# Pool's breaks, and the buffers of output rows and row weights, in a one-core FFT and expert kernel

## The chip, the cores and the metric

The kernel runs on one core of a Trainium2 chip. The metric is device time in microseconds, the median of several executions. The core has five engines that run side by side and wait for one another by semaphores: TensorE (PE, matrix products into PSUM), VectorE (DVE), ScalarE (ACT), GpSimd (POOL, called Pool below) and SyncE (SP). SP issues most of the DMAs. Pool issues the indirect ones, whose target rows are read from a table of indices.

## The reference, cut to what matters

```python
X = np.fft.fft(np.fft.fft(x, axis=1), axis=2).real      # x: 8 x 2496 x 256
x = X.reshape(19968, 256)
logits = x @ w_gate                                     # 8 experts
e_idx = np.argmax(logits, axis=1)
gate_w = softmax(logits)[arange, e_idx]
eom = 1.0 / (1.0 + np.exp(-(x @ w_output_gate)))
for e in range(8):
    mask = e_idx == e
    h = np.maximum(x[mask] @ w1[e], 0.0)                # 256 -> 1024
    out[mask] = gate_w[mask, None] * eom[mask, e, None] * (h @ w2[e])   # 1024 -> 256
```

Each of 8 batches is transformed along both axes. Every resulting row goes to the one expert with the largest logit, through two matrix products, and back to its own place, scaled by its gate weight.

## The kernel before, in words

**The background** transforms the batches one by one: chunks of x are loaded (tile `xt`), folded on DVE, multiplied by tables on PE (`dstage`, line 546, and `sstage`, line 573), and gathered in one of two buffers, `rowbuf`. `gating` (line 640) picks the expert and the position of each row. Then `scatter` (line 736) writes the rows into a DRAM scratch, sorted by expert: 20 indirect DMAs of 128 rows for each batch, issued by Pool. Each row carries its weight and its token number behind its 256 values.

**The foreground** is 93 slots (`sched`, line 1224) of up to 256 rows of one expert. `load_x_` (line 1321) has SP load a slot's rows transposed (`xr`) and then its row weights and token numbers (`xf`, tile name of `f`, line 1329). `mm1` makes the hidden values in four parts g, `mm2` follows three parts later (LAG) and makes the output: ACT scales it into `y` (line 1469), and Pool writes `y` to the output rows by indirect DMA (line 1471), which reads the token numbers out of `f`. So a buffer of `y` and one of `f` are free again only when that DMA has landed. Slots 0 to 43 take rows of the first six batches (in groups that need 2, 4 and 6 batches); the others come after all 8. Loads run two slots ahead of the work. The first four slots (n < KS) multiply in float32: DVE first adds the two halves of `xr` into `x32` (line 1390, `x` in the rows), which every `mm1` of that slot reads. Later slots use float16 pairs, with the expert's weights split by `conv` (line 1354) on ACT and DVE.

**Order.** SP and Pool execute in the order in which the program emits their work (`PH1`, line 93), up to the point at which the background is through; there is one queue each, so an instruction that waits holds up all behind it. The order on PE, ACT and DVE is chosen by a planner when the program is built, by its own cost table and with the same buffer waits; on the chip it is fixed. On Pool the 20 scatters of a batch are interleaved with the outputs of the slots: those of the fourth batch between the outputs of slots 0, 1 and 2 (6, 6 and 8 of them, line 1474), later ones about four to a slot. Those of the eighth batch stand in a list that is emptied step by step (line 1554), and four DMAs of padding rows follow them.

**Pool's breaks.** Two kinds stand between its DMAs. `zeros` (line 438) is two additions on a tile of zeros; `breath` (line 443) calls it before a DMA when four (RUN) have gone by since the last break. The other is a one-element memset into a row of `rowbuf` that has just been scattered (line 747): it must wait until that scatter has landed. `pauses` (line 734) says behind which scatters it stands; it also starts the count of `breath` anew. Between the third and the fourth batch `zeros` follows every third scatter.

**Pools of buffers.** `fx` is a list of pools: one until the background is through, then two. So `bufs=4 * len(fx)` is 4 buffers first and 8 later. Tiles with one tag in one pool take its buffers in turn, in the order in which they are made. `y` has its tag with 2 buffers, `x32` one of its own with 1.

Of the kernel before, what the change touches and what calls it, by code (L numbers as in the profile page):

```python
# [12 lines left out]
F32 = mybir.dt.float32  # L13
# [30 lines left out]
BA = BAS[0]  # L44
# [43 lines left out]
BH = 4  # L88
# [166 lines left out]
def fft_moe_kernel(ctx: ExitStack, tc: tile.TileContext, xl, wg, w1, w2, tde, tdo, gt, ts0, tsm, tsr, tsq, cst, tid, out):  # L255
# [44 lines left out]
    def whole(p, m, h):  # L300
        t = p[0][m][h]
        return t if p is raw else t.rearrange("p a n -> p (a n)").bitcast(F32)

    if True:
# [335 lines left out]
        def gating(b):  # L640
# [90 lines left out]
                last["tid"] = nc.scalar.copy(r[:, :, 1].bitcast(I32), tidt[P, b * 20 + 4 * i:b * 20 + 4 * i + 4])  # L731
                yield

            pauses = ((9, 19), (19,))[b] if b < BA else (1, 5, 9, 13, 17) if b >= BH else ()

            def scatter(j):
                if b >= BH:
# [325 lines left out]
        def route(b):  # L1063
            for _ in gating(b):
                pass
# [74 lines left out]
        def steps():  # L1140
            fc = 6 * KC
            for n in range(5 * NB):
                b, i = divmod(n, 5)
                if i == 0 and b > BH:
                    add_gen(gating(b - 1))
# [51 lines left out]
                if b == BH:  # L1197
                    fold(n + 5)
                yield ("step", n)
            add_gen(gating(NB - 1))  # L1200
            while gens:
                for _ in piece("C"):
# [7 lines left out]
    if True:  # L1210
        fx = []
# [98 lines left out]
        def entry(n, k, hi):  # L1310
            rd, qi = sched[n][:2]
            t, w = (slots_a + [slots_b])[rd], (NAS + [NQ])[rd]
            return nc.sync.value_load(t[0:1, k * w + qi:k * w + qi + 1], min_val=0, max_val=hi)

        def early(k, i):
            i_ = getattr(i, "ins", i)
            tc.add_to_no_dep_group(f"early_read{k}", i_)
            tc.declare_no_dep(i_, group=f"late{k}", reason="rows of other batches")
            return i

        def load_x_(n):
            rd, qi, N, _, off, _ = sched[n]
            U = (N + 127) // 128
            need(rd)
            begun.add(rd)
            a = sl_[n] = {"U": U, "N": N, "wb": wof[n]}
            r = rowat[n] if n < 2 else entry(n, 1, DUM - off)
            x = a["x"] = fx[-1].tile([128, 4, 256], F16, name="xr", tag="xr", bufs=3 * len(fx))
            f = a["f"] = fx[-1].tile([128, 2, 2], F32, name="xf", tag="xf", bufs=4 * len(fx))
            H = UNIT if N <= UNIT else 128  # L1330
            rows = scr[ds(r + off if off else r, H * U), :]
            for i in (nc.sync.dma_start_transpose(x[:, :, 0:H * U], rows[:, 0:D].bitcast(F16)),
                      nc.sync.dma_start(f[0:H, 0:U], rows[:, D:RW].rearrange("(u p) w -> p u w", p=H))):
                if rd < LAST:
                    early(rd, i)
            return i
# [29 lines left out]
        def psum(tag):  # L1366
            if "old" not in psf:
                return psf["h"]
            turn[tag] += 1
            own, kept_there = {"h": (3, 2), "y": (2, 1)}[tag]  # L1370
            there = turn[tag] % (own + kept_there) >= own
            psf["hb"], psf["yb"] = (2, 1) if there else (3, 2)
            return psf["old"] if there else psf["h"]

        def halves(a, h):
            t = fx[-1].tile([128, 4, 256], F32, name="hc", tag="hc", bufs=3 * len(fx))
            a["h", h] = t
            a["hh", h], a["hl", h] = (v for v in t.rearrange("p f t -> p (f t)").bitcast(F16).rearrange("p (a f t) -> a p f t", a=2, f=4))

        def mm1(n, g):  # L1380
            a = sl_[n]
            T = slice(0, a["N"])
            if g % 2 == 0:
                halves(a, g // 2)
            ps = psum("h").tile([128, 2, 256], F32, name="hp", tag="h", bufs=psf["hb"])
            if n < KS:
                if g == 0:
                    a["x32"] = fx[0].tile([128, 2, 256], F32, name="x32", tag="x32", bufs=1)
                    with tc.issue_after(last["x32" if n else "rt"].ins):
                        last["x32"] = nc.vector.tensor_tensor(a["x32"], a["x"][:, 0:2], a["x"][:, 2:4], op=ALU.add)  # L1390
                w = whole((raw, wbuf)[n % 2], 0, g // 2).rearrange("p (k f) -> p k f", k=2)
                for k in range(2):
                    f = (2 * g + k) % 4
                    for kc in range(2):
                        last["mm"] = nc.tensor.matmul(ps[:, k, T], w[:, kc, f * 128:(f + 1) * 128], a["x32"][:, kc, T], start=(kc == 0), stop=(kc == 1))
                last["hl"] = nc.scalar.activation(a["h", g // 2][:, 2 * (g % 2):2 * (g % 2) + 2, T], ps[:, :, T], AF.Relu)
                return
            w1v = wbuf[a["wb"]][0][g // 2].rearrange("p a (k f) -> p a k f", k=2)
            for k in range(2):
                f = 2 * g + k  # L1400
                m = 0
                for kc in range(2):
                    for hl, x in ((0, kc), (0, 2 + kc), (1, kc)):
                        last["mm"] = nc.tensor.matmul(ps[:, k, T], w1v[:, hl, kc, (f % 4) * 128:(f % 4 + 1) * 128], a["x"][:, x, T], start=(m == 0), stop=(m == 5))  # L1404
                        m += 1
            G = slice(2 * (g % 2), 2 * (g % 2) + 2)
            hh, hl = a["hh", g // 2], a["hl", g // 2]
            nc.scalar.activation(hh[:, G, T], ps[:, :, T], AF.Relu)  # L1408
            last["hl"] = nc.vector.scalar_tensor_tensor(hl[:, G, T], ps[:, :, T], 0.0, hh[:, G, T], op0=ALU.max, op1=ALU.subtract)  # L1409

        def mm2(n, g):
            a = sl_[n]
            U, h = a["U"], g // 2
            M = min(128, a["N"])
            if g == 0:
                a["yp"] = psum("y").tile([128, 2, 256], F32, name="yp", tag="y", bufs=psf["yb"])
                a["y"] = fx[0].tile([128, 2, 256], F32, name="y", tag="y", bufs=2)
                a["ys"] = fx[0].tile([128, 2], F32, name="ysc", tag="ysc", bufs=2)
            u = g % 2 if U == 2 else 0
            if n < KS:  # L1420
# [56 lines left out]

        def experts():
            chained(load_x_, 0)
            chained(load_x_, 1)  # L1480
            for h in range(2):
                conv(0, 0, h)
# [4 lines left out]
            for n in range(NS + 1):  # L1487
                while due <= n + (4 if LAST in ready else 2):
                    chained(load_x_, due)
                    due += 1  # L1490
# [5 lines left out]
                for g in range(4):  # L1496
                    if n < NS:
                        mm1(n, g)
                        yield "h"

                    k, j = divmod(4 * n + g - LAG, 4)
                    if 0 <= k < NS:
                        mm2(k, j)
                        yield "y"
# [66 lines left out]
    def need(i):  # L1571
        while i not in ready:
            next(bg, None)
# [66 lines left out]
```

## Time and profile before

| | |
|---|---|
| median of 3 runs | 1088.9 us (1084.75 to 1096.11) |
| the profiled execution | 1094.69 us, span 1092.9 us, mean granted clock 0.99 |
| PE busy | 1053.3 us, 96% of the span |
| DVE busy | 782.8 us, 72% |
| ACT busy | 700.0 us, 64% |
| Pool busy | 443.0 us, 41% |

The busy time of an engine is the time in which an instruction of it was executing; matrix products are pipelined and their ends are modelled, so that a PE that is busy throughout may still run at a lower clock. The granted clock is told as a share of full speed. What an engine waited for is inferred from semaphore events; a Pool DMA's own time is that of its issue, and its landing is later.

### The profile page before, as it was taken

How to read it: one execution, taken by the hardware profiler on the slowest of the kernel's cores; microseconds unless marked ns; L12 is line 12 of the kernel's file. 1: busy time of each engine (PE TensorE's matmuls, PEld its weight loads, DVE VectorE, ACT ScalarE, POOL GpSimd, SP SyncE). 2: the span in 40 equal slices, each digit the busy share in tenths (PEclk: the TensorE clock that was granted, in tenths of full speed). 3: DMA queues.
4: the chain of work that ended last, by engine and by line, in shares of the span. 5: the costliest groups of instructions: out<-in, count | busy, mean ns of one | idle time of the engine just before them, and what ended most of it. 6: DMA issues, size and time to landing. Idle time of an engine off the chain costs nothing.

```text
span 1092.9 us, 27037 instructions
## 1 busy us (share of the span) xinstructions
PE 1053.3 (96%) x9946; PEld 938.5 (86%) x9946; DVE 782.8 (72%) x1583; ACT 700.0 (64%) x1247; POOL 443.0 (41%) x435
## 2 busy tenths in 40 slices
PE   7979999989999999989988999999999999999997
PEld 6867888878999999978877888899999888888886
DVE  7877875889997585895443545588767778788873
ACT  3986765656876565545434554577767677778772
POOL 0067786723466645656554221231222222232322
PEclk9999999999999999999998999999999999999999
DMA  9947799855457555558568625697988988899820
GB/s 358 405 172 283 240 395 310 295 162 158 135 155 187 142 156 152 138 152 205 142 170 196 154 45 132 198 294 242 286 222 250 253 222 218 239 267 246 223 63 30
DMA packets 167388, 226.53 MB, mean 207 GB/s; under 512 B 117077, under 2 KB 117849, under 8 KB 167254
## 3 DMA queue, kind: packets, MB, share of 16 engines
q1 hardware_dynamic: 151046, 179.94, 59.4%
q0 software_dynamic: 16208, 44.85, 11.8%
q8 instruction: 78, 1.28, 0.5%
q14 instruction: 56, 0.46, 0.1%
HBM read 183.89 MB, written 43.80 MB: 208 GB/s over the span
## 4 chain that ended last, share of the span: by engine, by line
PE 72%; DMA 7%; issue 6%; POOL 6%; ACT 4%; DVE 4%; another core or an unknown queue 0%; POOLq 0%; SPq 0%; DVEq 0%; ACTq 0%
PE hp L1404 31%; PE yp L1442 30%; PE psb_t L600 6%; POOL scr L740 3%; PE psb_t L555 2%; DMA scr<-rowbuf,desti 2%; DMA xt<-in_xl_dram 2%; POOL out_dram L1471 1%; POOL ztile L440 1%; PE yp L1437 1%; DMA tstr<-in_tsr_dram 1%; DMA xt<-in_w_dram 1%; DMA out_dram<-y,xf 1%; PE psb_t L559 1%; ACT xt L414 0%
## 5 line engine op out<-in xcount | busy, mean ns | idle before, releaser
L1404 PE MATMUL hp<-xr,w0b 128*128 128x256 f16 (+5 forms) x4272 | 449.6, 256 | 8.6 <-DVE hc L1409 8.6
L1442 PE MATMUL yp<-w1b,hc 128*128 128x256 f16 x3480 | 431.8, 274 | 5.0 <-ACT y L1469 4.7
L1404 PEld LDWEIGHTS <-w0b 128*128 128x128 f16 x4272 | 365.7, 98 | 52.7 <-DVE hc L1409 9.7
L1471 POOL DMA_INDIRECT out_dram<-y,xf x166 | 200.9, 1210 | 454.0 <-ACT y L1469 407.8
L1442 PEld LDWEIGHTS <-hc 128*128 128x128 f16 x3480 | 337.4, 98 | 45.8 <-issue 5.2
L1408 ACT ACTIVATE hc<-hp 128x512 f16<-128x512 f32 (+6 forms) x356 | 184.2, 526 | 127.4 <-PE hp L1404 119.3
L1409 DVE SCALAR_TENSOR_TENSOR hc<-hp,hc 128x512 f16<-128x512 f32 (+6 forms) x356 | 209.1, 600 | 71.9 <-ACT hc L1408 65.9
L1361 DVE SCALAR_TENSOR_TENSOR w1b<-raw1b,ssc,w1b 128x1024 f16<-128x1024 f32 x124 | 160.3, 1292 | 76.4 <-ACT w1b L1360 61.7
L740 POOL DMA_INDIRECT scr<-rowbuf,desti x160 | 179.9, 1124 | 73.9 <-issue 53.9
L1361 DVE SCALAR_TENSOR_TENSOR w0b<-raw0b,ssc,w0b 128x1024 f16<-128x1024 f32 x124 | 159.8, 1289 | 65.7 <-ACT w0b L1360 44.9
L1360 ACT ACTIVATE w0b<-raw0b,ssc 128x1024 f16<-128x1024 f32 x124 | 141.9, 1146 | 45.5 <-PE hp L1404 31.8
L1360 ACT ACTIVATE w1b<-raw1b,ssc 128x1024 f16<-128x1024 f32 x124 | 141.9, 1145 | 31.8 <-PE yp L1442 15.2
L1469 ACT ACTIVATE y<-yp,ysc 128x256 f32<-128x256 f32 x145 | 61.1, 470 | 59.9 <-PE yp L1442 31.9
L555 PE MATMUL psb_t<-tdet,ft 128*125 128x290 f32 (+1 forms) x240 | 65.6, 427 | 5.7 <-DVE eo L627 2.8
L555 PEld LDWEIGHTS psb_t<-tdet,ft 128*125 128x125 f32 (+1 forms) x240 | 46.1, 197 | 21.1 <-issue 3.4
L440 POOL TENSOR_TENSOR ztile<-ztile 128x256 f32<-128x256 f32 x70 | 53.2, 761 | 4.6 <-DMA scr<-ztile,pidx 1.4
L600 PE MATMUL psb_t<-amid,tstq 125*128 125x145 f16 (+3 forms) x480 | 48.0, 255 | 2.7 <-ACT w0b L414 2.7
L1448 DVE TENSOR_SCALAR ysc<-xf,ssc 128x2 f32<-128x2 f32 (+5 forms) x89 | 19.8, 223 | 28.0 <-DMA xf<-scr 15.3
L475 DVE TENSOR_TENSOR xt<-xt 128x500 f32<-128x500 f32 (+1 forms) x40 | 27.1, 680 | 15.5 <-DMA xt<-in_xl_dram 11.6
L637 ACT COPY rowbuf<-rowbuf 128x508 f16<-128x508 f16 x40 | 24.5, 614 | 21.0 <-DVE rowbuf L634 14.8
L634 DVE TENSOR_TENSOR rowbuf<-rt,rowbuf 128x516 f16<-128x516 f32 x40 | 28.6, 716 | 12.2 <-ACT rowbuf L633 6.7
L600 PE MATMUL psb_t<-amid,tst 128*128 128x145 f16 (+2 forms) x320 | 32.2, 251 | 2.5 <-ACT amid L567 2.5
(234 smaller groups left out, 843.1 us busy)
## 6 DMA issues: line engine op xcount, KB each, us to landing
raw0b<-in_w_dram SPq DMA_DIRECT2D x130, 512.0 KB
raw1b<-in_w_dram SPq DMA_DIRECT2D x130, 512.0 KB
xt<-in_xl_dram SPq DMA_DIRECT2D x40, 512.0 KB
xt<-in_w_dram SPq DMA_DIRECT2D x16, 512.0 KB
w0b<-in_w_dram SPq DMA_DIRECT2D x6, 512.0 KB
w1b<-in_w_dram SPq DMA_DIRECT2D x6, 512.0 KB
out_dram<-y,xf POOLq DMA_INDIRECT x166
scr<-rowbuf,desti POOLq DMA_INDIRECT x160
```

The lines of the kernel that those rows point to most:

```text
L440: nc.gpsimd.tensor_tensor(ztile[:, 0:D], ztile[:, 0:D], ztile[:, 0:D], op=ALU.add)
L555: last["ds"] = nc.tensor.matmul(o[:, 0:290], ft[:, j, par, W], tdw[:, j], start=(j == 0), stop=(j == 1))
L600: last["pe"] = nc.tensor.matmul(ps[:, k, c0:c0 + 145], tab[hl][K, t], a[K, kc, par, c0:c0 + 145], start=(n == 0), stop=(n == len(terms) - 1))
L740: free_order("scr", batch=b, inst=nc.gpsimd.indirect_dma_start(out=scr[:, :], out_offset=bass.IndirectOffsetOnAxis(ap=desti[:, j:j + 1], a ...
L1360: nc.scalar.activation(w[:, 0], r, AF.Copy, scale=sc)
L1361: nc.vector.scalar_tensor_tensor(w[:, 1], r, sc, w[:, 0], op0=ALU.mult, op1=ALU.subtract)
L1404: last["mm"] = nc.tensor.matmul(ps[:, k, T], w1v[:, hl, kc, (f % 4) * 128:(f % 4 + 1) * 128], a["x"][:, x, T], start=(m == 0), stop=(m == 5))
L1408: nc.scalar.activation(hh[:, G, T], ps[:, :, T], AF.Relu)
L1409: last["hl"] = nc.vector.scalar_tensor_tensor(hl[:, G, T], ps[:, :, T], 0.0, hh[:, G, T], op0=ALU.max, op1=ALU.subtract)
L1442: nc.tensor.matmul(a["yp"][0:M, u], a[k, h][:, f, u * 128:u * 128 + M], w2v[:, hl, f], start=(g == 0 and f == 0 and m == 0), stop=(h == 1 ...
L1469: nc.scalar.activation(a["y"][0:M, u], yp, AF.Copy, scale=ys[0:M, u:u + 1])
L1471: free_order("out", nc.gpsimd.indirect_dma_start(out=out[:, :], out_offset=bass.IndirectOffsetOnAxis(ap=a["f"].bitcast(I32)[0:M, u, 1:2], ...
```

## The change

Four lines are edited. From the fifth batch on there are no memsets behind scatters, so the only breaks are those of `breath`, one pair of additions before every fifth DMA. `f` has 8 buffers from the start. `y` has 3 buffers, and `x32` now takes its buffers from the same tag: for the first slots the buffers are taken in the order x32 of slot 0, y of slot 0, x32 of slot 1, y of slot 1, x32 of slot 2 and so on, with three in turn. So x32 of slot 2 takes the buffer that held y of slot 0, and x32 of slot 3 that of y of slot 1.

```diff
-            pauses = ((9, 19), (19,))[b] if b < BA else (1, 5, 9, 13, 17) if b >= BH else ()
+            pauses = ((9, 19), (19,))[b] if b < BA else ()
...
-            f = a["f"] = fx[-1].tile([128, 2, 2], F32, name="xf", tag="xf", bufs=4 * len(fx))
+            f = a["f"] = fx[-1].tile([128, 2, 2], F32, name="xf", tag="xf", bufs=8)
...
-                    a["x32"] = fx[0].tile([128, 2, 256], F32, name="x32", tag="x32", bufs=1)
+                    a["x32"] = fx[0].tile([128, 2, 256], F32, name="x32", tag="y", bufs=3)
...
-                a["y"] = fx[0].tile([128, 2, 256], F32, name="y", tag="y", bufs=2)
+                a["y"] = fx[0].tile([128, 2, 256], F32, name="y", tag="y", bufs=3)
```

Here BA is 2, BH is 4 and KS is 4; the batches count from 0.

## Rows read from the trace of the kernel before

**Rows 1.** The page: busy time by engine, and the chain that ended last.

```profile
PE 1053.3 (96%) x9946; PEld 938.5 (86%) x9946; DVE 782.8 (72%) x1583; ACT 700.0 (64%) x1247; POOL 443.0 (41%) x435
PE 72%; DMA 7%; issue 6%; POOL 6%; ACT 4%; DVE 4%; another core or an unknown queue 0%; POOLq 0%; SPq 0%; DVEq 0%; ACTq 0%
```

**Rows 2.** Busy us (instructions) of each engine by stretch; granted clock, DMA share, GB/s.

```profile
225.00:250.00 25.00, 21.72 (x166) 17.84 (x165) 21.74 (x53) 14.93 (x26) 5.62 (x4) 0.93 0.52 158
...
575.00:600.00 25.00, 22.51 (x179) 18.74 (x179) 10.38 (x14) 11.11 (x18) 9.88 (x11) 0.86 0.85 197
...
625.00:650.00 25.00, 25.00 (x231) 22.41 (x230) 13.03 (x18) 12.35 (x18) 4.93 (x4) 1.00 0.31 55
```

**Rows 3.** ACT's timeline, 440 to 600 us: start, us, [idle before, releaser].

```profile
525.36 0.84 ACT L1469 ACTIVATE y<-yp,ysc 128x256 f32<-128x256 f32 x2 [0.71 <-PE yp L1442]
...
576.60 0.84 ACT L1469 ACTIVATE y<-yp,ysc 128x256 f32<-128x256 f32 x2 [6.56 <-DMA out_dram<-y,xf]
...
598.86 0.84 ACT L1469 ACTIVATE y<-yp,ysc 128x256 f32<-128x256 f32 x2 [0.71 <-PE yp L1442]
```

**Rows 4.** Waits, 460 to 600 us: us in total, times, longest.

```profile
ACT y L1469 <- DMA out_dram<-y,xf: 15.9, 5, 6.6
...
DVE ysc L1448 <- DMA xf<-scr: 14.7, 5, 7.0
...
SPq L1333 <- DMA out_dram<-y,xf: 80.2, 10, 13.6
```

**Rows 5.** PE's timeline, 540 to 600 us.

```profile
577.49 6.49 PE L1442 MATMUL yp<-w1b,hc 128*128 128x256 f16 x32 [3.65 <-ACT y L1469]
```

**Rows 6.** Pool's instructions by line and form: busy us, mean ns, idle before.

```profile
L1471 POOL DMA_INDIRECT out_dram<-y,xf x166 | 200.9, 1210 | 454.0 <-ACT y L1469 407.8 <-issue 18.3 <-DMA raw0b<-in_w_dram 7.3
L740 POOL DMA_INDIRECT scr<-rowbuf,desti x160 | 179.9, 1124 | 73.9 <-issue 53.9 <-DVE desti L708 16.5 <-DVE r_t L824 1.1
L440 POOL TENSOR_TENSOR ztile<-ztile 128x256 f32<-128x256 f32 x70 | 53.2, 761 | 4.6 <-DMA scr<-ztile,pidx 1.4
...
L747 POOL MEMSET rowbuf<- 1x1 f32 x23 | 2.0, 88 | 74.4 <-DMA scr<-rowbuf,desti 74.4
```

**Rows 7.** Pool's timeline, 120 to 420 us.

```profile
148.95 0.99 POOL L740 DMA_INDIRECT scr<-rowbuf,desti  x1 [0.16 <-issue]
...
153.98 0.99 POOL L740 DMA_INDIRECT scr<-rowbuf,desti  x1 [0.15 <-issue]
...
162.95 0.97 POOL L1471 DMA_INDIRECT out_dram<-y,xf  x1 [0.30 <-ACT sq L513]
...
182.49 1.39 POOL L1471 DMA_INDIRECT out_dram<-y,xf  x1 [0.30 <-issue]
```

**Rows 8.** All engines' timeline, 223 to 240 us.

```profile
229.49 0.69 DVE L475 TENSOR_TENSOR xt<-xt 128x512 f32<-128x512 f32 x1 [2.35 <-DMA xt<-in_xl_dram]
...
238.19 2.19 PE L1404 MATMUL hp<-xr,w0b 128*128 128x256 f16 x11 [3.01 <-DVE hc L1409]
```

**Rows 9.** The chain that ended last, in order of time: start, us, what.

```profile
219.43 5.18 DMA out_dram<-y,xf
...
574.06 2.43 DMA out_dram<-y,xf
```

**Rows 10.** DVE's timeline, 125 to 232 us.

```profile
159.14 0.68 DVE L1390 TENSOR_TENSOR x<-xr 128x512 f32<-128x512 f16 x1
```

**Rows 11.** PE's timeline, 125 to 235 us.

```profile
161.22 1.89 PE L1395 MATMUL hp<-x,raw0b 128*128 128x256 f32 x8
...
183.60 1.94 PE L1395 MATMUL hp<-x,w0b 128*128 128x256 f32 x8
```

**Rows 12.** All engines' timeline, 484 to 520 us.

```profile
516.78 1.72 DVE L1361 SCALAR_TENSOR_TENSOR w1b<-raw1b,ssc,w1b 128x1024 f16<-128x1024 f32 x1 [0.64 <-issue]
...
517.43 2.23 POOL L440 TENSOR_TENSOR ztile<-ztile 128x256 f32<-128x256 f32 x2
```

**Rows 13.** The page: the costliest groups, mean ns of one.

```profile
L1361 DVE SCALAR_TENSOR_TENSOR w1b<-raw1b,ssc,w1b 128x1024 f16<-128x1024 f32 x124 | 160.3, 1292 | 76.4 <-ACT w1b L1360 61.7
```

## The prediction

> **What bounds the kernel now.** I read the page first. PE is busy for 96% of the span and holds 72% of the chain that ended last; Pool holds 6% and DMAs 7% [rows 1]. So a change can win only what PE idles or runs slowly, about 40 us of idle time (1092.9 minus 1053.3), and only where Pool or a landing DMA causes it. The table by stretch shows where. From 600 us on PE is full: 231 products in 25 us, 108.2 ns each; 575 to 600 us has 179 at a mean granted clock of 0.86, and 225 to 250 us has 0.93 [rows 2].
>
> The reader's key rows are ACT's scalings into `y`. A slot has 96 products, so it should take 96 x 108.2 ns = 10.39 us. Between the scalings at 525.36 and 598.86 us there are six slots in 73.50 us [rows 3], where 62.3 would do: 11.2 us are lost. The waits name the cause: between 460 and 600 us ACT waits 15.9 us for output DMAs to land (one of the two `y` buffers must come free), SP stands 80.2 us at the load of `xf` for the same landings (one of four `f` buffers), and DVE waits 14.7 us for the `xf` that SP loads late [rows 4]. At 577.49 us this reaches PE: it stands for 3.65 us, and its next 32 products take 6.49 us where 32 x 0.1082 = 3.46 are due [rows 5]. That is the lower of its two clock levels (1.2 GHz) for most of them, after an idle stretch.
>
> Pool is late because of what a slot costs it. Four scatters and two outputs take 6 x (1.15 in the mean + the 0.30 that stands before each) = 8.7 us, a pair of additions 1.5 us, and a landing wait with its memset (74.4 + 2.0)/23 = 3.3 us: 13.5 us, against PE's 10.39 [rows 6, 7]. Earlier slots are stretched by background work on PE and leave Pool time; from about 500 us on they are not.
>
> **The change, part by part.**
>
> *The landing waits.* Of the 23 memsets 20 go (five for each of four batches); they cost Pool some 20 x 3.3 = 66 us. What comes instead: 80 scatters, 4 pads and about 50 outputs of slots 6 to 30 stand under the count, and one pair for four DMAs makes 33 pairs, where the trace has 20 in that stretch: 13 more, 13 x 1.52 = 20 us. A slot's six DMAs with 1.5 pairs then take 8.7 + 2.5 = 11.2 us by the means. By Pool's undisturbed pace it is less: three scatters and a pair take 5.03 us (148.95 to 153.98) without any landing wait [rows 7], so a pair adds 5.03 - 3 x 1.28 = 1.2 us, and a slot takes 7.7 + 1.8 = 9.5 us. Against 10.39 Pool stays level or falls back by 0.8 us a slot for the six slots in which the last 24 scatters and pads are interleaved, 5 us in all.
>
> *Third `y` buffer, eight `f` buffers.* These 5 us are covered: a third buffer gives an output one more slot, 10.4 us, to land, and eight buffers of `f` give four more slots. Without that cover the 5 us would come back at ACT. So the ACT, SP and DVE waits of [rows 4] should go, and with them the 11.2 us: I take **-11**. Bounds: -7 if Pool's lag still costs two slots 2 us each, and -14.5 if a loss of about 3.5 us before 500 us, which PE has behind DVE, goes as well. Next late is then PE itself.
>
> *`f` again, at 220 us.* The load of slot 7's `xf` waits for the output of slot 3, which landed 5.18 us after its issue at 219.43 [rows 9]. The chunks of x queued behind it on SP come late: DVE stands 2.35 us for one at 229.49, and PE stands 3.01 us behind DVE at 238.19 [rows 8], at a mean clock of 0.93 around it, worth 0.07 x 25 = 1.8 us [rows 2]. With eight buffers nothing waits there. Bounds -2.4 (what DVE waited) and -4.8; I take **-3**, near the DVE wait, since DVE stays behind with other work.
>
> *`x32` in `y`'s tag.* This adds a wait. DVE's addition of slot 2 ran at 159.14 us [rows 10]; now it must wait until slot 0's output has landed. Pool issues the second half of that output at 162.95, behind the third batch's scatters [rows 7], which the change leaves alone. Outputs land 2.43 to 5.18 us after their issue [rows 9], here at 165.4 to 168.1. With 0.68 for the addition, slot 2's first product can start at 166.1 to 168.8 instead of 161.22 [rows 11]: 4.9 to 7.6 us later. Slot 3 waits likewise for slot 1's output, issued until 182.49 [rows 7]: 185.6 to 188.4 instead of 183.60, 2.0 to 4.8 us. Behind the addition stand DVE's folds and evictions for batches 4 and 5, and PE waits for those too. But PE has slot 1's second product and the background's tables in the same stretch, and the planner knows of the wait and can put them first. Lower end 0 (covered), upper end 7.6 plus 3.0 for the low clock afterwards = 10.6. I take **+4**, nearer to the covered end.
>
> *More additions beside DVE.* A weight split that met a pair took 1.72 us [rows 12], where its mean is 1.29 [rows 13]. Thirteen pairs at 0.43 are 5.6 us of DVE's time. In the Pool-bound stretch DVE is busy for 10.38 of 25 us [rows 2], which hides it there. Bounds 0 and 2 on PE; I take **+0.5**. The Trainium skill, page "SBUF — State Buffer", section "Who interferes with whom", says that a DVE instruction with two SBUF inputs contends with a GpSimd instruction that reads SBUF, and that whoever comes second is blocked for the whole instruction. By that rule the additions speak against this change; the rows agree that both lengthen, but show a third of the full block.
>
> **Sum.** -11 - 3 + 4 + 0.5 = -9.5. The profiled execution took 1094.69 us, so its like would take 1085.2. It lies above the median of 1088.9 and within the runs' spread; I count from the median: **1079.4 us**, rounded 1079.
>
> **The rivals.**
>
> 1. *The early wait eats the gain.* The planner's idea of when slot 0's output lands is wrong on the chip, the order is fixed, and PE stands 7.6 us and then runs slowly: -14 + 10.6 + 0.5 = -3, 1086 us. For it: Pool is in scatters until just before 162.95 us [rows 7], and DVE's queue holds the background's work too. Against: the fillers named. 0.18.
> 2. *Slower: both waits in full.* Slots 2 and 3 both stand, 7.6 + 4.8, with 3.0 of low clock after each: +18.4, so -14 + 18.4 + 0.5 = +5, 1094 us. It decides once the two stalls exceed 13.5 us together. Against: if slot 2 slips, slot 3 is due later and its wait is partly over. 0.13.
> 3. *More than forecast.* The early wait is covered, and the 3.5 us before 500 us go too: -14.5 - 4.8 + 0.5 = -19, 1070 us. 0.15.
> 4. *Additions block DVE fully.* If 13 x 1.52 = 20 us of DVE reach PE in the stretches where DVE is nearly full: -14 + 4 + 20 = +10, 1099 us. It is the rule of "SBUF — State Buffer" in the Trainium skill taken at its word. Against: the 1.72 above, and DVE's 72% [rows 1]. 0.04.
> 5. *Pool stays the bound.* Issues lengthen without landing waits, or landings do, and half of the late loss stays: -5.5 - 3 + 4 + 0.5 = -4, 1085 us. Against: the pace of 5.03 us for three scatters and a pair without a landing wait [rows 7]. 0.05.
>
> **How the numbers follow.** The forecast has 0.45, with its own range from 1074 to 1085 (the bounds of its terms, not all at one end). Rivals 3, 1, 2, 5 and 4 follow with the chances given. The range 1068 to 1095 takes in 1 to 3 and 5 and leaves out rival 4, the far ends and surprises of a newly planned order, under 2 in 10. About 1% is what a measurement of this kernel can tell from no change, 1078.0 to 1099.8 here. Faster than that: rival 3 and about half of the forecast, 0.15 + 0.23, with a little of the others 0.40. Slower: half of rival 4, the tail of rival 2 and a bad new order, 0.07. Within: 0.53.
>
> **What would show it.** Right, if ACT's wait for output DMAs and SP's at the load of `xf` between 460 and 600 us fall to near zero; if slots from 500 us on come every 10.4 us and the granted clock there is 1.00; if Pool shows idle time before outputs, waiting for ACT, where it now has landing waits; and if the stop at 238 us shrinks. The early step shows in DVE's addition of slot 2: later than 165 us with PE still full around it if covered, PE idle for 5 us or more, with a clock below 1, if not. Wrong, above all, if PE's busy time between 150 and 200 us falls by over 8 us, or if Pool's output DMAs still trail ACT by more than two slots at 560 us.

## The result, and the profile after

The changed kernel took **1077.07 us** in the median (1075.33 to 1079.06), the kernel before 1090.24 beside it (1084.75 to 1096.11). The ratio is **0.987**, with an interval from 0.983 to 0.9911. The forecast was 1079, so time and range held; the reasons held only in part. The profiled execution took 1076.54 us with a span of 1074.7: 18.2 us less than the span before. The medians differ by 13.2 only, because the profiled run of before lies 4.5 us above its median.

The page of after, busy time by engine and the chain that ended last [rows 1]:

```profile
PE 1047.2 (97%) x9946; PEld 937.2 (87%) x9946; DVE 776.2 (72%) x1583; ACT 703.0 (65%) x1247; POOL 408.7 (38%) x375
...
PE 89%; DVE 4%; ACT 3%; DMA 2%; issue 1%; POOL 0%; SPq 0%; POOLq 0%; DVEq 0%; ACTq 0%
```

Pool has left the chain (6% before), DMAs hold 2% of it instead of 7%, and PE holds 89%. Pool has 60 instructions fewer, which comes back below. The table by stretch of after, with the same columns as [rows 2]:

```profile
225.00:250.00 25.00, 24.27 (x201) 20.92 (x200) 24.55 (x61) 16.87 (x27) 4.12 (x4) 1.00 0.45 129
575.00:600.00 25.00, 25.00 (x230) 22.17 (x229) 11.38 (x15) 12.21 (x18) 4.93 (x4) 1.00 0.71 161
625.00:650.00 25.00, 25.00 (x232) 22.40 (x230) 13.25 (x17) 12.89 (x19) 5.82 (x5) 1.00 0.30 83
```

Both weak stretches are mended: 201 products at a granted clock of 1.00 where there were 166 at 0.93, and 230 where there were 179 at 0.86. ACT's timeline of after, the scalings of the same three slots as [rows 3]:

```profile
517.40 0.84 ACT L1469 ACTIVATE y<-yp,ysc 128x256 f32<-128x256 f32 x2 [0.71 <-DMA scr<-rowbuf,desti]
...
570.31 0.47 ACT L1469 ACTIVATE y<-yp,ysc 128x256 f32<-128x256 f32 x1 [0.71 <-PE yp L1442]
...
580.79 0.47 ACT L1469 ACTIVATE y<-yp,ysc 128x256 f32<-128x256 f32 x1 [0.71 <-PE yp L1442]
```

The six slots take 63.39 us instead of 73.50. Of the waits between 460 and 600 us, the rows of [rows 4] are gone; PE, Pool and SP's queue now head their lists with these, in total, times, longest:

```profile
PE hp L1404 <- DVE hc L1409: 0.5, 1, 0.5
...
POOL out_dram L1471 <- ACT y L1469: 63.9, 13, 8.5
...
SPq L1351 <- DVE w1b L1361: 33.2, 12, 5.3
```

Pool waits for ACT, as forecast, and SP's queue for weight buffers. Pool by line and form, for [rows 6]:

```profile
L1471 POOL DMA_INDIRECT out_dram<-y,xf x166 | 206.9, 1246 | 551.4 <-ACT y L1469 509.2 <-DMA raw0b<-in_w_dram 8.6 <-ACT w1b L1360 7.9
L740 POOL DMA_INDIRECT scr<-rowbuf,desti x160 | 173.1, 1082 | 64.7 <-issue 43.7 <-DVE desti L708 16.5 <-DVE rt L631 1.1
L440 POOL TENSOR_TENSOR ztile<-ztile 128x256 f32<-128x256 f32 x30 | 21.2, 705 | 1.5
...
L747 POOL MEMSET rowbuf<- 1x1 f32 x3 | 0.3, 88 | 4.7 <-DMA scr<-rowbuf,desti 4.7
```

Here is the surprise. The 20 memsets went, but **so did 40 of the 70 additions** [rows 6]: from the fifth batch on Pool has no break at all. The code says why. `breath()` puts a pair in where `run["n"] == RUN` while `run["on"]` is set, and then counts on. Outputs count too, also before `run["on"]`. Before, a memset set the count back to 0 now and then; now it has passed four when `run["on"]` is set, and never equals four again. The prediction had counted 33 pairs, 13 more than before.

The span by stage, in us, from ACT's scalings as above (slots counted from 0; the step from slot 8 to 9 is left out), for all kernels but noadds and bare, which the next section explains with the others:

```
            slot 0   0-4    4-5    5-8   9-20   20-26  26-32  32-end
before      154.28  70.46  18.38  54.79  146.31  67.57  73.50  494.07
after       155.81  68.10  13.99  55.48  146.31  64.07  63.39  493.88
y_only      158.81  68.88  16.39  55.26  146.66  66.49  68.36  494.02
f_only      161.92  70.25  13.84  55.34  147.75  68.34  71.34  494.10
fy          159.16  68.69  13.81  55.59  146.80  68.92  65.42  494.01
p_only      156.65  68.71  16.75  55.80  157.24  67.77  64.73  494.43
p_again     155.10  69.47  17.44  54.99  156.36  70.87  64.82  494.22
pf          156.41  70.25  13.71  55.68  146.31  64.07  63.40  493.95
py          156.42  67.52  18.14  54.86  146.31  64.08  63.40  493.90
p_breaks    157.17  70.24  17.10  54.76  148.87  67.46  63.40  493.94
breaks      158.49  68.68  13.71  56.82  148.88  66.05  63.39  493.87
x32_wait    163.11  69.97  15.03  53.84  157.98  70.12  64.06  494.00
```

Each row is one execution. The first column and 0-4 vary by several us between kernels that stand alike there; 9-20 and 26-32 repeat closely (146.31 in four kernels, 63.39 or 63.40 in five), so single microseconds are read from those two above all.

### The profile page after: what moved, and what is told of

Read it like the earlier page. It is cut to its first block, busy times and chain, and to the rows that moved or that the text cites. A ratio compares the mean times of both kernels' runs of the same rounds, so it can differ in the third digit from the quotient of the medians.

```text
span 1074.7 us, 26981 instructions
## 1 busy us (share of the span) xinstructions
PE 1047.2 (97%) x9946; PEld 937.2 (87%) x9946; DVE 776.2 (72%) x1583; ACT 703.0 (65%) x1247; POOL 408.7 (38%) x375
## 3 DMA queue, kind: packets, MB, share of 16 engines
q8 instruction: 78, 1.28, 0.5%
## 4 chain that ended last, share of the span: by engine, by line
PE 89%; DVE 4%; ACT 3%; DMA 2%; issue 1%; POOL 0%; SPq 0%; POOLq 0%; DVEq 0%; ACTq 0%
PE hp L1404 36%; PE yp L1442 34%; PE psb_t L600 7%; PE psb_t L555 3%; PE yp L1423 3%; PE hp L1395 2%; DMA xt<-in_xl_dram 1%; PE yp L1437 1%; DMA raw1b<-in_w_dram 1%; DVE xt L475 1%; DVE rowbuf L634 1%; PE psb_t L559 0%; ACT rowbuf L637 0%; PE psb_t L557 0%; DVE rt L631 0%
## 5 line engine op out<-in xcount | busy, mean ns | idle before, releaser
L1471 POOL DMA_INDIRECT out_dram<-y,xf x166 | 206.9, 1246 | 551.4 <-ACT y L1469 509.2
L740 POOL DMA_INDIRECT scr<-rowbuf,desti x160 | 173.1, 1082 | 64.7 <-issue 43.7
L555 PEld LDWEIGHTS psb_t<-tdet,ft 128*125 128x125 f32 (+1 forms) x240 | 45.1, 192 | 18.2 <-ACT rowbuf L637 3.3
L475 DVE TENSOR_TENSOR xt<-xt 128x500 f32<-128x500 f32 (+1 forms) x40 | 27.0, 680 | 13.2 <-DMA xt<-in_xl_dram 13.1
L637 ACT COPY rowbuf<-rowbuf 128x508 f16<-128x508 f16 x40 | 24.5, 613 | 18.3 <-DVE rowbuf L634 18.2
L633 ACT CAST rowbuf<-rt 128x516 f16<-128x516 f32 x40 | 25.0, 624 | 6.3 <-DMA scr<-rowbuf,desti 3.2
L600 PEld LDWEIGHTS psb_t<-amid,tstq 125*128 125x128 f32 (+1 forms) x192 | 25.8, 199 | 2.9 <-ACT w0b L414 2.7
```

The costliest lines, as they stand in the source:

```text
L555: last["ds"] = nc.tensor.matmul(o[:, 0:290], ft[:, j, par, W], tdw[:, j], start=(j == 0), stop=(j == 1))
L600: last["pe"] = nc.tensor.matmul(ps[:, k, c0:c0 + 145], tab[hl][K, t], a[K, kc, par, c0:c0 + 145], start=(n == 0), stop=(n == len(terms) - 1))
L740: free_order("scr", batch=b, inst=nc.gpsimd.indirect_dma_start(out=scr[:, :], out_offset=bass.IndirectOffsetOnAxis(ap=desti[:, j:j + 1], a ...
L1471: free_order("out", nc.gpsimd.indirect_dma_start(out=out[:, :], out_offset=bass.IndirectOffsetOnAxis(ap=a["f"].bitcast(I32)[0:M, u, 1:2], ...
```

## The experiments

They ran in three sets, each with its own runs of the kernel before: p_only, f_only, y_only and fy; then breaks, p_breaks, pf and py; then the rest. Theory L says that Pool's landing waits make the late loss; rival B, that too few buffers make it.

**p_only**: the landing waits out, nothing else.

```diff
-            pauses = ((9, 19), (19,))[b] if b < BA else (1, 5, 9, 13, 17) if b >= BH else ()
+            pauses = ((9, 19), (19,))[b] if b < BA else ()
```

> Only the landing waits behind scatters are taken out; f keeps 4 buffers, y keeps 2, x32 its own. Theory L (Pool's landing waits make the late loss, the buffers only cover a rest): the six slots scaled between 525 and 599 us in the kernel before come every 10.4 to 10.7 us instead of 12.25, about -10 us; the stop near 238 us, which comes from f, stays; total -10 to -14, ratio 0.987 to 0.991. Rival B (the number of buffers makes the loss, Pool's pace matters little): at most -3, ratio above 0.997.

Measured 1102.62 us, ratio 1.0092 (1.0051 to 1.0133): about 1% **slower**, a miss, since neither theory forecast a loss. Slots 26 to 32 behave as Theory L says (64.73). The loss is elsewhere: slots 9 to 20 take 10.9 us more. PE's timeline of p_only there:

```profile
446.70 0.29 PE L600 MATMUL psb_t<-amid,tstq 125*128 125x145 f16 x2 [1.09 <-issue]
447.44 0.48 PE L600 MATMUL psb_t<-amid,tstq 125*128 125x145 f16 x5 [0.45 <-issue]
448.19 0.30 PE L600 MATMUL psb_t<-amid,tstq 128*128 128x145 f16 x2 [0.27 <-issue]
...
449.63 1.01 PE L1442 MATMUL yp<-w1b,hc 128*128 128x256 f16 x4 [0.70 <-issue]
451.05 1.09 PE L1442 MATMUL yp<-w1b,hc 128*128 128x256 f16 x4 [0.41 <-issue]
452.48 0.39 PE L1442 MATMUL yp<-w1b,hc 128*128 128x256 f16 x1 [0.33 <-issue]
```

PE stops and starts in the middle of groups of one line, with no releaser that the trace knows ("issue"). Pool's timeline of p_only in the same stretch:

```profile
440.68 1.34 POOL L740 DMA_INDIRECT scr<-rowbuf,desti  x1 [0.30 <-issue]
...
450.31 1.24 POOL L740 DMA_INDIRECT scr<-rowbuf,desti  x1 [0.30 <-issue]
```

Eight scatters stand back to back from 440.68 to 451.55 us, and the last of PE's stops ends within 1 us of their end. Between 225 and 600 us such stops of PE are 8.3 us in all (350, 365, 416, 446 to 452, 482, 523 and 546 us), most of them beside or just behind a run of scatters. Before and after have none; f_only and fy, which keep all landing waits, have 0.9 us each.

**f_only**: eight buffers for `f`, nothing else.

```diff
-            f = ... tag="xf", bufs=4 * len(fx))
+            f = ... tag="xf", bufs=8)
```

> Only f has 8 buffers from the start; landing waits stay and y has 2 buffers. Theory L: slot 5 is scaled about 4.4 us earlier (the load behind the output of slot 3 no longer waits) and the last loss stays, because ACT still needs one of two y buffers; -4 to -8, ratio 0.992 to 0.996. Rival B: SP's 80 us at the load of xf were the cause, and most of the late 11 us goes as well: -12 or more, ratio 0.989 or less.

Measured 1090.99, 0.9962 (0.9934 to 0.999), at the edge of what was expected. Slot 4 to 5 takes 13.84 us instead of 18.38.

**y_only**: three buffers for `y`, with `x32` among them.

```diff
-                    a["x32"] = ... tag="x32", bufs=1)
+                    a["x32"] = ... tag="y", bufs=3)
-                a["y"] = ... tag="y", bufs=2)
+                a["y"] = ... tag="y", bufs=3)
```

> Only y has 3 buffers, with x32 in its tag; landing waits stay and f has 4 buffers. Theory L: Pool still needs 13.5 us for a slot that takes PE 10.4, so the third buffer only puts the loss off: half of the late 11 us stays and the stop near 238 us stays: -3 to -7, ratio 0.9935 to 0.997. Rival B: Pool's arrears are finite (24 scatters and pads), one more buffer outlasts them and the late loss is gone: -9 to -11, ratio 0.990 to 0.992.

Measured 1090.75, 0.9991 (0.9959 to 1.0022), less than expected. The late slots gain 5.1 us (68.36) and slots 0 to 4 lose none, yet the median shows nothing that can be told from no change.

**fy**: both buffer edits, landing waits kept.

> Both buffer changes, but the landing waits stay: the changed kernel without its first edit. Theory L: Pool falls 3 us a slot behind for six slots, 18 us against 10.4 of one more buffer: 5 to 8 us of the late loss stay, ratio 0.991 to 0.994 to the kernel before. Rival B: the buffers outlast Pool's arrears and nothing of the loss is left: ratio 0.984 to 0.988, as for the changed kernel.

Measured 1088.54, 0.9972 (0.9939 to 1.0006), less than expected again. The late slots gain 8.1 us by buffers alone (65.42): landing waits out or buffers in are two cures for the same loss, and only the first cures it whole.

**breaks**: after, with the count mended so that the pairs come.

```diff
-            if run["on"] and run["n"] == RUN:
+            if run["on"] and run["n"] >= RUN:
```

> After, with `run["n"] >= RUN` in place of `== RUN`: in the trace of after, Pool has no addition at all between 240 and 600 us (30 in the whole run against 70 before), since the count has passed four before `run["on"]` is set; with `>=` the pair of additions really comes after every four DMAs, 33 pairs in all, as the prediction counted. Theory S (spare time): Pool stands 169 us between 240 and 600 us waiting for outputs' scalings, 33 pairs at 1.5 us (50 us) fit in, time as after, 0.985 to 0.990 of before, DVE's weight splits back from 1.28 to about 1.31 us. Rival B (the additions cost DVE or put Pool behind): each pair that meets a split delays it, and Pool's outputs come late again from slot 25 on: +5 to +12 us on after, 0.992 to 0.998.

Measured 1086.16, 0.996 (0.9934 to 0.9985): rival B by its size, and in part by the first of its two reasons (a pair that meets a split delays it; how much of it was found stands under "More additions" below). Pool by form shows the pairs, 64 additions more than after:

```profile
L440 POOL TENSOR_TENSOR ztile<-ztile 128x256 f32<-128x256 f32 x94 | 73.3, 779 | 4.6 <-DMA scr<-ztile,pidx 0.3
```

The second reason, late outputs, is not it (26-32 is 63.39). PE's waits of breaks between 225 and 600 us:

```profile
PE hp L1404 <- DVE hc L1409: 4.9, 5, 2.2
PE psb_t L600 <- DVE amid L571: 1.8, 2, 1.6
PE yp L1442 <- DVE w1b L1361: 0.4, 1, 0.4
```

and of after:

```profile
PE hp L1404 <- DVE hc L1409: 1.2, 2, 0.7
PE yp L1442 <- DVE w1b L1361: 0.2, 1, 0.2
PE psb_t L600 <- DVE amid L571: 0.2, 1, 0.2
```

PE waits for DVE 7.1 us instead of 1.6, most of it at 266, 461 and 484 us, where DVE is nearly full (23.23 of 25 us from 250, 24.20 from 450, 22.40 from 475). Against pf and py of the same set, which have none of them, the 32 pairs cost 7 us.

**p_breaks**: the same edit on p_only, so without landing waits, with the old buffers and with pairs.

> p_only with `>=`, so without landing waits, with old buffers, but with a pair of additions after every four DMAs. In p_only PE stops 8 us in all with no releaser that the trace shows, each time while Pool sends scatters back to back (350, 365, 416, 446 to 452, 522 us), and its clock falls after the longest. Theory C (unbroken scatters stop PE): with the pairs in, those stops go to under 2 us in all, and p_only's 1.009 becomes 0.990 to 0.998. Rival D (the stops come from the order and buffers, not from unbroken scatters): stops stay at 5 us or more and the ratio stays at 1.003 to 1.010.

Measured 1088.3, 0.9945 (0.9915 to 0.9976), as theory C says: no stop of PE without a releaser, and 9-20 back to 148.87. It also tells buffers from waits, by ACT's timeline of p_breaks:

```profile
529.83 0.47 ACT L1469 ACTIVATE y<-yp,ysc 128x256 f32<-128x256 f32 x1 [0.71 <-PE yp L1442]
...
593.23 0.47 ACT L1469 ACTIVATE y<-yp,ysc 128x256 f32<-128x256 f32 x1 [0.71 <-PE yp L1442]
```

63.40 us with two `y`, four `f` and all pairs: the landing waits alone made the late loss. SP's queue still waits for outputs, and nothing is late for it:

```profile
SPq L1333 <- DMA out_dram<-y,xf: 39.3, 11, 5.5
```

Slots 20 to 26, however, take 67.46, as before (67.57); without pairs 64.07 in pf, py and after. So that gain hangs at least in part on the missing additions (breaks and after, which differ in nothing else, are 2.0 us apart there); taking out the landing waits alone does not bring it.

**pf** and **py**: p_only's edit with f_only's, and with y_only's.

> Landing waits out and eight f buffers; y stays at two and x32 has its own buffer. Theory C/D (p_only's stops have nothing to do with f): slot 5 comes 4.5 us earlier as in f_only, stops without a releaser stay in the order of 4 to 8 us, ratio 1.000 to 1.006. Rival F (SP standing at an f buffer is what harms p_only): stops under 2 us, and the ratio 0.986 to 0.991, all of the change's gain without y.

> Landing waits out and three y buffers with x32 among them; f stays at four. Theory C/D: stops stay, slot 5 as in before (no 4.5 us there), ratio 1.000 to 1.008. Rival Y (output buffers are what harms p_only): stops under 2 us, late loss (slots 26 to 31) at most 1.5 us, ratio 0.990 to 0.994.

Measured 1079.13, 0.9859 (0.9788 to 0.9929), and 1079.34, 0.9866 (0.9793 to 0.9938). Neither has a stop without a releaser, so both rivals came true at once, which neither had allowed: each buffer "heals" p_only, though Pool's and SP's orders are the same in p_only, pf and py. From 242 us on all five engines of the three have one and the same order, stops or not, so the order does not make the stops there. From slot 9 to 32 the stages agree with after to 0.02 us. The third `y` buffer shows no gain of its own beside pf.

**x32_wait**: after, but slot 2's `x32` lies where slot 0's `y` lay, so that it must wait for that output.

```diff
-                    a["x32"] = ... tag="y", bufs=3)
+                    a["x32"] = ... tag="y0" if n == 2 else "y", bufs=1 if n == 2 else 2)
-                a["y"] = ... tag="y", bufs=3)
+                a["y"] = ... tag="y0" if n % 3 == 0 else "y", bufs=1 if n % 3 == 0 else 2)
```

> After, with slot 2's x32 given the very buffer that y of slot 0 used (a tag of its own with one buffer for slot 2's x32 and the y of every third slot, two buffers for the other y), so that DVE's addition has to wait until slot 0's output has landed: the wait that the prediction priced at +4 us. In after the addition runs at 153.65 us and the output is issued at 162.54 and 163.82. Theory W (the prediction's wait, its price right): the addition comes at 165 to 169 us, PE has a gap or shifts, slots 2 on come 2 to 8 us later than in after: 0.989 to 0.995 of before. Rival 0 (covered by other products of PE): addition that late, but slots 4 on within 1.5 us of after, 0.985 to 0.989.

Measured 1101.24, 1.0068 (1.0042 to 1.0095): outside both. The order is now the one that the forecast had, `x32` behind slot 0's output, by the timelines of Pool and DVE of x32_wait:

```profile
167.73 0.97 POOL L1471 DMA_INDIRECT out_dram<-y,xf  x1 [0.30 <-issue]
...
176.77 1.28 DVE L1390 TENSOR_TENSOR x<-xr 128x512 f32<-128x512 f16 x2
```

but its table by stretch shows PE full beside it:

```profile
150.00:175.00 25.00, 25.00 (x117) 21.35 (x116) 17.72 (x54) 14.14 (x31) 20.66 (x24) 1.00 0.97 326
175.00:200.00 25.00, 25.00 (x190) 22.37 (x189) 13.64 (x48) 15.56 (x33) 15.43 (x17) 1.00 1.06 360
```

Slots 0 to 4 take 1.9 us more than in after, where rival 0 allowed 1.5 and kernels that stand alike differ by more. So rival 0 is about right on the late addition (covered), and the time went elsewhere: slot 0 comes 7.3 us later, before the wait acts, and 9-20 has the stops of p_only again (9.3 us on PE between 240 and 600 us), though it has eight `f` buffers and from 311 us on the order of after on every engine.

**p_again**: p_only unchanged.

> p_only once more, unchanged, on another day's share of a chip: its twins pf and py have the same order on Pool and SP and took 1079 us, while p_only took 1102.6 us with 8 us of stops on PE that have no releaser in the trace. Theory H (the stops belong to that chip's share of the time, not to the program): no stops, 0.986 to 0.994 here. Rival K (they belong to the kernel: two y and four f buffers together): stops of 5 us or more again, 1.004 to 1.013.

Measured 1098.6, 1.0047 (1.0019 to 1.0076), with 9.8 us of stops at the same places. The loss repeats, so it is not one set's alone, nor one chip's: p_again ran on the chip of pf and py. The expectation's reason K (two `y` and four `f` together) falls all the same, by x32_wait.

**noadds** and **bare**: after without any addition; and without the three landing waits of batches 0 and 1 as well.

```diff
-            for _ in range(2):
-                nc.gpsimd.tensor_tensor(ztile[:, 0:D], ztile[:, 0:D], ztile[:, 0:D], op=ALU.add)
             run["n"] = 0
```

> After without any of the remaining 15 pairs of additions (those of batches 2 and 3 beside the row scatters); the landing waits of batches 0 and 1 stay. The whole order is planned anew. Theory A (an addition costs DVE, as the 33 pairs of the kernel breaks did, 9 us or 0.27 us a pair): 0 to -4 us against after, 0.983 to 0.987. Rival N (in batches 2 and 3 the unbroken scatters delay transfers of x and weights, which bound that stage): +2 to +10 us, 0.989 to 0.996.

> noadds, and the three landing waits of batches 0 and 1 out as well, so Pool never pauses. Theory A: those three waits cost Pool 5 us where it has work waiting in the first 150 us, so -1 to -3 us against noadds. Rival N: transfers bound that stage, same as noadds or later by 2 us or more.

Measured 1139.31, 1.0434 (1.0369 to 1.0498), and 1154.83, 1.0565 (1.0514 to 1.0615): far worse than any theory had it. The order on PE, ACT and DVE is another one from 125 to some 470 us, so the sum isn't the additions' price alone. But up to 125 us every engine of noadds has the order of after, p_again and x32_wait, but for three pairs of additions in the second batch (the expectation put all 15 pairs into later ones), and that stretch shows the harm by itself. Pool's timeline of noadds (line numbers are two lower there):

```profile
95.32 0.98 POOL L738 DMA_INDIRECT scr<-rowbuf,desti  x1 [0.30 <-issue]
...
118.36 0.97 POOL L738 DMA_INDIRECT scr<-rowbuf,desti  x1 [0.30 <-issue]
```

nineteen scatters with gaps of 0.31 us at most; and PE's timeline of noadds:

```profile
119.24 6.00 PE L553 MATMUL psb_t<-tdet,ft 128*125 128x290 f32 x14 [17.87 <-issue]
```

with ACT's and DVE's waits of noadds, 100 to 125 us:

```profile
ACT rowbuf L635 <- issue: 17.9, 1, 17.9
...
DVE p_x L292 <- remote: 17.7, 1, 17.7
```

PE, ACT and DVE stand together, in the middle of their work, and start again in the last 3 us of Pool's run. Of the two kernels of the same set that have the three pairs, p_again has no such stop of PE in that stretch, and x32_wait three of 1.7 us at most. Full DMA engines alone are not the cause: their share is 1.02 in the stop (101 to 116 us) and also in p_again from 95 to 110 us, where PE is busy for 12.45 of 15 us. Nor does a stop always last until the run ends: in the next twenty scatters of noadds, from 141.30 us, PE stands from 150.63 us and starts again with four still to come:

```profile
161.98 5.15 PE L1393 MATMUL hp<-x,raw0b 128*128 128x256 f32 x16 [11.36 <-issue]
166.49 3.44 POOL L738 DMA_INDIRECT scr<-rowbuf,desti  x1 [0.30 <-issue]
```

## Why the prediction held, and where it failed

**The landing waits: -11 forecast, -10.1 found** in slots 26 to 32. Right in size and cause. Wrong in the reason given for the buffers: the step "Without that cover the 5 us would come back at ACT" fails, since p_breaks has the old buffers and all the pairs and loses nothing. Pool's lag of 0.8 us a slot did not come about there. (By the forecast's own 1.52 us a pair, 1.5 pairs are 2.3 us and not 2.5, and the lag would have been 0.6.)

**The 3.5 us before 500 us: taken as 0, a bound only; found -3.5** (67.57 to 64.07). The forecast's bound was the right size, but at least 2.0 us of it come from the additions that vanished: with pairs in, p_breaks has 67.46 there and breaks 66.05.

**`f` at 220 us: -3 forecast, -3.7 found.** Slot 4 to 5 fell by 4.4 us, of which 0.7 are given back by slot 8. In every kernel of the table with eight `f` buffers that step takes 15.1 us or less, with four 16.3 or more (bare, with eight and the stops, takes 16.1). PE's stop shrank from 3.01 us [rows 8] to

```profile
234.64 1.49 PE L1404 MATMUL hp<-xr,w0b 128*128 128x256 f16 x12 [0.73 <-DVE hc L1409]
```

**`x32` in `y`'s tag: +4 forecast, about 0 found.** This step failed twice. DVE's timeline of after:

```profile
153.65 0.70 DVE L1390 TENSOR_TENSOR x<-xr 128x512 f32<-128x512 f16 x1
...
178.41 0.68 DVE L1390 TENSOR_TENSOR x<-xr 128x512 f32<-128x512 f16 x1
```

and Pool's:

```profile
162.54 0.97 POOL L1471 DMA_INDIRECT out_dram<-y,xf  x1 [0.30 <-issue]
163.82 1.19 POOL L1471 DMA_INDIRECT out_dram<-y,xf  x1 [0.31 <-ACT xt L414]
```

Slot 2's addition runs 5.5 us *earlier* than in [rows 10], before slot 0's output is even issued: it cannot have waited for it. That fits buffers that go round in the planned order of their tiles: `x32` of slot 1 is added at 135.18 us, ahead of slot 0's scaling at 155.81, so that slot 2 takes over slot 0's `x32` and not its `y`. The forecast, and the account of the change ahead of it, had them in the order of the slots. And where x32_wait enforces the wait, PE has other products and slots 0 to 4 lose 1.9 us, which is within what that column varies by: the covered end of the bounds was nearer than +4. Rivals 1 and 2, which rested on this wait, fall with it.

**More additions: +0.5 forecast.** There were 40 fewer, not 26 more; that the change didn't do what it says was not among the rivals. What pairs cost when they come was measured in breaks: 7 us for 32 pairs against none. The step priced 13 more than 20; their share of the 7 us would be some 3 us, an estimate, above the +0.5 and the upper bound of 2. The step failed at "hides it there": it looked at the Pool-bound stretch, where DVE is busy for 10.38 of 25 us, while the pairs hurt where DVE is nearly full. Rival 4 (10 us slower, all 20 us of additions on PE) thus had the right engine and too high a price. Of breaks' weight splits between 230 and 600 us, 13 overlap a pair and take 1.54 us in the mean, the other 57 take 1.28; the longest took 2.07. That is 0.26 us a meeting, and 3 us in all; the rest of the 7 us was not traced to single meetings, so its cause is not shown. The Trainium skill, page "SBUF — State Buffer", section "Who interferes with whom", has the second of the two blocked for the whole instruction; one addition takes 0.78 us, so the longest split (0.79 over 1.28) fits a whole block, and the mean is a third of one, as the forecast had it.

**The sum.** Forecast -9.5. Found in the profiled spans: -10.1 - 3.5 - 3.7 - 0.8 (up to slot 4) - 0.2 (after slot 32) = -18.3, against 18.2 measured. In medians it is -13.2. That the number came within 2.3 us of the forecast is in part luck: two harms that it counted (+4 and +0.5) did not happen, and additions that vanished unforeseen gave 2 us or more. By the traces the forecast is 9 us short; the medians hide 5 us of that, because the profiled runs of before and after lie 4.5 us above and 0.5 below theirs. Rival 3, with its -19, described the trace better than the forecast, though its 1070 us is 7 below the measured median.

**What stays open.** PE's stops beside unbroken scatters came in p_only, p_again, x32_wait, noadds and bare, and not in after, pf and py, which have the same runs of up to eight scatters. The two groups were also timed in different sets, so for these runs kernel and set can't be told apart: after was not run in a set in which the stops occurred, and p_breaks' cure is a comparison across sets. That f_only and fy, in the set of p_only, have 0.9 us of stops despite their landing waits, while no kernel in the set of pf has any, speaks for the set. For the twenty scatters of the second batch the comparison is within one set and one order, and there the missing additions make the stop, by one profiled execution of each kernel. By what resource Pool's run holds up the others, no view shows. No kernel tried beat the changed one.

## What to carry to other kernels

Look for the wait that one engine's queue makes all others stand behind before adding buffers: here taking out twenty waits cured what more buffers only eased. Check in the trace that an inserted pause or spacer is really there; a counter compared with `==` had lost 40 instructions without a word. And let no long run of DMA issues from Pool go unbroken on trust: short breaks cost 7 us here; without them three kernels lost nothing, two (p_only, run twice, and x32_wait) had 8 to 10 us of stops, and noadds and bare, with runs of twenty, stops of up to 18 and 12 us at a time.

## What the runs showed of the hardware

Scatters from Pool with nothing between them can stop PE, ACT and DVE together, with no releaser in the trace: PE stood 17.9 us in one run of twenty in noadds, until the run ended, and 11.4 us in the next, which went on. With a pair of additions after every fifth scatter, in the same order and the same set, PE's stops were at most 1.7 us. In runs of up to eight the stops were 8 to 10 us in all in p_only, p_again and x32_wait, and none in after, pf and py. An addition on Pool lengthens the DVE split that it meets by 0.26 us in the mean (1.28 to 1.54). And two executions of kernels with the same early order can differ by over 7 us at slot 0 already (154.28 in before, 161.92 in f_only).
